# Two-layer products and seven-product groups in one stream on TensorE: the order of the units, a third waiting item and a fourth rotating bank

## The chip, the cores and the metric

The kernel runs on one core of a Trainium2 chip. The metric is the device time of one execution in microseconds (us). A core has TensorE (PE, matrix products; PEld is its weight load, which runs beside the products), VectorE (DVE), ScalarE (ACT), GpSimd (POOL) and SyncE (SP, which here issues most DMA transfers). Each engine works through its own instructions in the order in which they are written for it, and waits on semaphores for the others. Products are summed in PSUM, of which the kernel has eight banks of 128 x 512 fp32.

## The reference

```
X = fft(fft(x, axis=1), axis=2).real          # 8 batches of 3072 x 256
e = argmax(X @ w_gate)                        # one of 8 experts for each of 24576 tokens
y = scale * (relu(X @ w1[e]) @ w2[e])         # w1: 256 x 1024, w2: 1024 x 256
out = relu(y @ w_in) ** 2 @ w_out             # w_in: 256 x 2048, w_out: 2048 x 256
```

`scale` is the gate's probability times a sigmoid. All of it is fp32. The kernel splits every operand into a high and a low part (h and l) and forms each product as three: h by h, h by l, l by h.

## The kernel before

**Slots.** The Fourier transforms of the eight batches run first and scatter their tokens, sorted by expert, into a buffer `xs`. The rest works on slots of 256 tokens of one expert: 48 full ones (F) of the last window, 40 of earlier windows, and the tail slots (T), in which the experts' remainders lie. A unit is one slot's work in the first two layers; its output `y` is a tile of 128 x 512. The last window has 60 units, 48 F and 12 T, after batch eight.

**First two layers** (`items_a`, lines 634 to 668). Four items a unit. Each is `mm1` (12 products of 128x128 by 128x256 into a bank `ph`), `evac` (ACT relu into `hh`, DVE remainder `hl`) and `mm2` (12 products into `py`). After the fourth, ACT copies `py` to `ys`.

**The other two layers.** For the windows before the last: `items_c`, eight items a slot, relu and square (`squares`, lines 812 to 821), 12 products into `po`. In the last window two F slots make a pair, and `items_s` (line 753) computes the pair's third layer with seven products in place of eight (Strassen's way): eight steps, each `one` (12 products into two banks `px` and `pz2`, ACT copies `m`, DVE sums `u`, `z`, `x` on line 778), `two` (nine more products into the same banks, then `squares` on both) and two `last` (12 products each into `po`). That is 45 products a step, 360 a group. `inputs` (line 738) builds the group's operands `bh`, `bl` from two `ys`. The tail slots' outputs are summed up in DRAM (`yt`) and read back as four groups of two slots.

**Order.** The units of the last window are 24 F, then twelve times F, T, F. For each unit the loop in `run` first pushes the four items of the first two layers, then a share of the steps of the group whose slots came before. `push` lets `lag` = 2 items wait for their second half; `push_group` runs `one`, one waiting item, `two`, and leaves at most three waiting. A scheduler then moves single products among neighbours. After the last unit come `beyond` (line 940: a branch, not taken here, on the number of tail slots, PE's row L944), the last pair, and the four groups of tail slots with no first layers beside them.

**Weights.** An expert's `w1` and `w2` (1 MB each) land in single buffers `r1` and `r2`, issued by SP (lines 570 and 571) when the last split has read the buffer, and only when the expert changes (`chg`). `split_w(k)` (lines 582, 583) makes chunk k of four: ACT casts to `w1h` and `w2h`, POOL forms `w1l` and `w2l`. These too are single buffers, so that a cast for the next unit waits until PE has used the chunk. The load for the next unit stands in front of a unit's four items, the splits between the group steps behind them.

**Banks.** `ph`, `px` and every second `pz2` share three banks with the tag h; the other `pz2` have a bank of their own (tag fd). `py`, two `po` and one for transposes take the rest.

Of the kernel before, what the change touches and what calls it, by code (L numbers as in the profile page):

```python
# [10 lines left out]
F32 = mybir.dt.float32  # L11
# [3 lines left out]
U32 = mybir.dt.uint32  # L15
# [84 lines left out]
class Kern:  # L100
    def __init__(self, tc, a, B):
        self.tc, self.nc, self.a, self.B = tc, tc.nc, a, B
        self.L = B * S + SLOT
        self.sc_b, self.loads, self.outs = set(), False, False
        self.queue, self.lag, self.last_w = [], 2, None
        self.strassen = False
# [398 lines left out]
    def changes(self, *exs):  # L505
# [3 lines left out]
        if len(exs) == 1:  # L509
            m = exs[0]  # L510
        else:
            m = wp.tile([1, n], F32, name="exm", bufs=1)

            f, t = exs
            g = t.shape[1]
            h = f.shape[1] - 2 * g
            r = m[:, h:n].rearrange("p (g k) -> p g k", k=3)
            if h:
                v.tensor_copy(out=m[:, 0:h], in_=f[:, 0:h])
            v.tensor_copy(out=r[:, :, 0:3:2], in_=f[:, h:].rearrange("p (g k) -> p g k", k=2))  # L520
            v.tensor_copy(out=r[:, :, 1], in_=t)
# [86 lines left out]
    def ids(self, ids, scales):  # L608

        i = self.ap.tile([P, 2], U32, name="id", bufs=6)  # L610
        s = self.ap.tile([P, 2], F32, name="sc", bufs=6)
# [8 lines left out]

    def first(self, wh, wl, x, chunk):

        ph = self.ps.tile([P, 512], F32, name="ph", tag="h", bufs=3)
# [10 lines left out]
    def items_a(self, sl):  # L634
        st = {}
        for i in range(4):
# [10 lines left out]
            def mm2(i=i):  # L647
# [10 lines left out]
                if i == 3:  # L658
                    if self.strassen:
                        ys = self.yp.tile([P, 2, SLOT], F32, name="ys", tag="yl" if sl["tail"] else "yh", bufs=2)  # L660
# [92 lines left out]
    def items_s(self, b, ids):  # L753
# [10 lines left out]
        for g in range(8):  # L764
# [57 lines left out]

    def push_group(self, it):
        one, two, *last = it
        one()
        if self.queue:
            self.queue.pop(0)()
        two()
        self.queue += last
        while len(self.queue) > 3:  # L830
            self.queue.pop(0)()
# [18 lines left out]
    def run(self, units):  # L850
# [40 lines left out]
        groups = []  # L891
        for u in units[len(single):]:
            if not groups or (sum(not x["tail"] for x in groups[-1]) == 2 and not u["tail"]):
                groups.append([])
            groups[-1].append(u)
        self.strassen = True
        work = [(1, it) for it in self.items_c(pend)]
        first = True
        for group in groups:
            for k, u in enumerate(group):  # L900
                nxt = after.get(id(u))
                if nxt:
                    self.load(nxt) if "tab" in nxt else (nxt["open"](nxt), self.load(nxt))
                for it in self.items_a(u):
                    self.push(it)
                    yield
                n = -(-len(work) // (len(group) - k))
                part, work = work[:n], work[n:]
                todo = [lambda q=q: self.split_w(q) for q in range(4)] + [lambda: self.prep(nxt)] if nxt else []
                for q, (kind, it) in enumerate(part):  # L910
                    (self.push if kind == 1 else self.push_group)(it)
                    for _ in range(len(todo) if q == len(part) - 1 else kind if q else kind - 1):
                        if todo:
                            todo.pop(0)()
                    yield
                if first:
                    first = False
                    self.sums()
            pair = [u for u in group if not u["tail"]]
            while "y" not in pair[1]:  # L920
                self.queue.pop(0)()
            work = [(2, it) for it in self.items_s(self.inputs(pair[0]["y"], pair[1]["y"]), [u["id"] for u in pair])]
        self.flush()
        self.beyond(next(u["tab"] for u in units if u["tail"]))
        for kind, it in work:
            self.push_group(it)
        for m in range(self.n_tail // 2):
            y = [self.yp.tile([P, 2, SLOT], F32, name="ys", tag="yh", bufs=2) for _ in range(2)]
            ids = []
            for q in range(2):  # L930
                at = (2 * m + q) * SLOT
                self.nc.sync.dma_start(out=y[q], in_=self.yt[:, :, at:at + SLOT])
                raw = self.ap.tile([P, 2, 2], F32, name="rawid", bufs=2)
                self.nc.sync.dma_start(out=raw, in_=self.idt[at:at + SLOT, :].rearrange("(t p) o -> p t o", p=P))
                ids.append(self.ids(raw[:, :, 0], raw[:, :, 1]))
            for it in self.items_s(self.inputs(*y), ids):
                self.push_group(it)
        self.flush()
# [20 lines left out]
def build(ctx, tc, a, B, plan, pace=1.25):  # L959
# [54 lines left out]
    for w, (nb, n) in enumerate(plan):  # L1014
        kinds = [False] * n
        if w == len(plan) - 1:
            kinds = [False] * (n - 2 * KEEP) + [False, True, False] * KEEP
# [50 lines left out]
```

## Time and profile before

| what | value |
| --- | --- |
| median of three runs | 3784.23 us (3779.04 to 3785.14) |
| the profiled execution | 3785.43 us, its span 3783.8 us |
| PE, PEld | 3605.2 us (95%), 3528.7 us (93%) |
| ACT, DVE, POOL | 2412.7 us (64%), 2120.9 us (56%), 1585.8 us (42%) |
| DMA | 226.35 MB in packets, mean 60 GB/s |

PE's row in the page counts a matmul as busy until its modelled end, about 0.28 us after its start, while the next one starts about 0.12 us after it. Pauses shorter than that do not show as idle time. So this document measures PE by its count of matmuls: a stretch without any wait gives the time from one start to the next, and what a stretch takes beyond its count times that is pause. The last window's work on PE begins at about 1775 us. From there to about 2610 us the units are F alone, then F, T, F to about 3520 us, then the branch, the last pair and the four tail groups; the last store ends the span.

### The profile page before, as it was taken

Reading aid. Unit: us, or ns where it says so; the run is one execution under the profiler, and the core shown is the slowest. Engines: PE = TensorE matmul, PEld = TensorE weight load, DVE = VectorE, ACT = ScalarE, POOL = GpSimd, SP = SyncE. Lnnn points to the kernel's source line nnn. Section 1 sums busy time; section 2 is a strip of 40 time slices with the busy share of each in tenths; the row PEclk is TensorE's granted clock in tenths of the full one; section 3 lists DMA queues with packets and bytes.
Section 4 is the critical chain, followed back from the end, with each engine's and each line's share of the span. In section 5 each row is a group of like instructions: output and inputs, shape, how many; then the busy total and the mean of one; then the engine's idle time right before and its main releaser. Section 6 shows DMA issues by size and latency. Waiting matters only on the chain. (4 is left out here: it accounts for less than half of the span.)

```text
span 3783.8 us, 76706 instructions
## 1 busy us (share of the span) xinstructions
PE 3605.2 (95%) x29484; PEld 3528.7 (93%) x29484; DVE 2120.9 (56%) x4043; ACT 2412.7 (64%) x4793; POOL 1585.8 (42%) x1612
## 2 busy tenths in 40 slices
PE   4599999999999998999999999999999999999998
PEld 4588999999999998999999999999999999999888
DVE  8776666767676766333445545445444445444554
ACT  3455666665656565666667767767666677767565
POOL 4755455455444544333433433333544444444100
PEclk9799999999999999999999999999999999999999
DMA  5314222212121311011010101012221102100000
GB/s 188 131 50 135 65 95 83 93 65 90 60 96 38 109 47 63 16 66 37 22 34 15 40 15 39 20 57 65 79 99 64 45 29 81 64 21 18 24 24 12
DMA packets 157811, 226.35 MB, mean 60 GB/s; under 512 B 18560, under 2 KB 128384, under 8 KB 157440
## 3 DMA queue, kind: packets, MB, share of 16 engines
q1 hardware_dynamic: 137920, 166.46, 13.9%
q0 software_dynamic: 19520, 54.94, 4.0%
q8 instruction: 233, 3.82, 0.4%
q14 instruction: 138, 1.13, 0.1%
HBM read 288.79 MB, written 56.29 MB: 91 GB/s over the span
## 5 line engine op out<-in xcount | busy, mean ns | idle before, releaser
L618 PE MATMUL po<-woh,hl 128*128 128x256 f32 x3072 | 871.0, 285 | 28.1 <-DVE hl L820 28.1
L618 PE MATMUL po<-woh,hh 128*128 128x256 f32 x3072 | 864.1, 282 | 18.5 <-ACT hh L819 17.2
L618 PE MATMUL po<-wol,hh 128*128 128x256 f32 x3072 | 860.1, 281 | 4.2 <-POOL wol L411 4.2
L583 POOL TENSOR_TENSOR w1l<-r,w1h 128x512 fp32r<-128x512 f32 x400 | 523.7, 1313 | 727.9 <-ACT w1h L582 726.8
L583 POOL TENSOR_TENSOR w2l<-r,w2h 128x512 fp32r<-128x512 f32 x400 | 524.0, 1316 | 297.5 <-ACT w2h L582 284.6
L618 PEld LDWEIGHTS po<-woh,hl 128*128 128x128 f32 x3072 | 579.7, 189 | 48.3 <-DVE hl L820 48.0
L618 PEld LDWEIGHTS po<-woh,hh 128*128 128x128 f32 x3072 | 581.6, 189 | 20.9 <-ACT hh L819 19.3
L618 PEld LDWEIGHTS po<-wol,hh 128*128 128x128 f32 x3072 | 581.6, 189 | 5.0 <-POOL wol L411 4.9
L644 DVE SCALAR_TENSOR_TENSOR hl<-ph,hh 128x512 fp32r<-128x512 f32 x400 | 274.1, 688 | 439.6 <-ACT hh L643 438.8
L582 ACT CAST w1h<-r 128x512 fp32r<-128x512 f32 x400 | 246.7, 622 | 404.7 <-PE ph L618 382.7
L618 PE MATMUL py<-hl,w2h 128*128 128x256 f32 x1600 | 454.3, 284 | 16.0 <-DVE hl L644 15.8
L618 PE MATMUL ph<-xl,w1h 128*128 128x256 f32 x1600 | 456.1, 285 | 7.2 <-DVE xl L590 7.2
L618 PE MATMUL ph<-xh,w1h 128*128 128x256 f32 x1600 | 455.4, 285 | 1.2 <-ACT w1h L582 1.2
L618 PE MATMUL ph<-xh,w1l 128*128 128x256 f32 x1600 | 452.8, 283 | 1.4 <-POOL w1l L583 1.4
L618 PE MATMUL py<-hh,w2l 128*128 128x256 f32 x1600 | 451.4, 282 | 0.4 <-POOL w2l L583 0.4
L618 PE MATMUL py<-hh,w2h 128*128 128x256 f32 x1600 | 449.6, 281 | 0.0
L820 DVE TENSOR_TENSOR hl<-ph,hh 128x512 fp32r<-128x512 f32 x320 | 220.1, 688 | 375.9 <-ACT hh L819 375.7
L820 DVE TENSOR_TENSOR hl<-px,hh 128x512 fp32r<-128x512 f32 x224 | 155.0, 692 | 463.5 <-ACT hh L819 428.2
L618 PE MATMUL ph<-yh,wih 128*128 128x256 f32 x1280 | 369.5, 289 | 0.0
L618 PE MATMUL ph<-yl,wih 128*128 128x256 f32 x1280 | 360.7, 282 | 0.0
L618 PE MATMUL ph<-yh,wil 128*128 128x256 f32 x1280 | 360.7, 282 | 0.0
L815 ACT ACTIVATE rl<-ph 128x512 f32<-128x512 f32 x320 | 191.8, 600 | 256.4 <-PE ph L618 249.8
(279 smaller groups left out, 9822.3 us busy)
## 6 DMA issues: line engine op xcount, KB each, us to landing
r<-w SPq DMA_DIRECT2D x198, 1024.0 KB
xr<-xs SPq DMA_DIRECT2D x100, 260.0 KB
trig<-c_trig SPq DMA_DIRECT2D x104, 128.0 KB
X<-x SPq DMA_DIRECT2D x8, 1024.0 KB
X<-x SPq DMA_DIRECT2D x8, 768.0 KB
X<-x SPq DMA_DIRECT2D x8, 640.0 KB
conv<-w_in SPq DMA_DIRECT2D x16, 256.0 KB
conv<-w_out SPq DMA_DIRECT2D x16, 256.0 KB
```

The costliest lines, as they stand in the source:

```text
L582: nc.scalar.copy(out=h, in_=r)
L583: nc.gpsimd.tensor_tensor(out=l, in0=r, in1=h.bitcast(F32), op=ALU.subtract)
L618: self.nc.tensor.matmul(out=out, lhsT=l, rhs=r, start=first and i == 0, stop=last and i == len(pairs) - 1, skip_group_check=True)
L644: self.evac = self.nc.vector.scalar_tensor_tensor(out=l, in0=st[i], scalar=0.0, in1=h.bitcast(F32), op0=ALU.max, op1=ALU.subtract)
L815: self.nc.scalar.activation(out=r, in_=ps, func=AF.Relu)
L820: self.evac = self.nc.vector.tensor_tensor(out=l, in0=ps, in1=h.bitcast(F32), op=ALU.subtract)
```

## The change

1. `lag` is 3 instead of 2, for the whole kernel.
2. The units of the last window are twelve times F, T, F first, then 24 F.
3. Behind the first three units, pushes and `push_group` give way to `weave`: in each step of a group it writes `one`, the first waiting `last` of the step before, one `mm1`, `two`, the second `last` with any further `mm1`, and then the evacuation and `mm2` of the items taken. A plan says how many items a step takes. In the F, T, F part it is two ahead of the group and then 1, 2, 1, 1, 1, 2, 1, 1; in the F part two ahead and then 0, 1, 0, 1, 0, 1, 0, 1.
4. `stream` brings the weights: the load for the unit after the next one is written right behind a unit's fourth item, and each of the next unit's four splits behind an item's `mm2`.
5. `bank` gives `ph`, `px` and `pz2` four banks in rotation (three of tag h and fd).
6. `beyond` stands in the middle, between the F, T, F part and the F part. Before it the items in flight are finished; behind it the first unit's weights are loaded without a condition and split anew. The four tail groups stand between the pairs of the F part; the last pair alone has no first layers beside it.
7. `id` and `sc` get 10 buffers instead of 6, `ys` of odd slots a second tag, the tail groups' inputs the buffers of `ot`; the table of expert changes follows the new order.

The products are the same in number. The core of the diff (the bookkeeping in `changes` and `kinds`, and the code that goes out of `run`, left out):

```
-        self.queue, self.lag, self.last_w = [], 2, None
+        self.queue, self.lag, self.last_w = [], 3, None
...
+    def bank(self, name):
+        self.turn = (self.turn + 1) % 4 if self.woven else 0
+        tag, bufs = ("fd", 1) if self.turn == 3 else ("h", 3)
+        return self.ps.tile([P, 512], F32, name=name, tag=tag, bufs=bufs)
...
-                x = self.ps.tile([P, 512], F32, name="px", tag="h", bufs=3)
-                z = self.ps.tile([P, 512], F32, name="pz2", tag="fd" if g % 2 else "h", bufs=1 if g % 2 else 3)
+                x, z = self.bank("px"), self.bank("pz2")
...
+        for q in range(KEEP - 1):
+            self.weave(groups(q), a, [2] + [1, 2, 1, 1, 1, 2, 1, 1])
...
         self.beyond(next(u["tab"] for u in units if u["tail"]))
+        self.last_w = None
+        rest = late[3 * KEEP:]
+        a = self.stream(rest, True)
...
+            if m < self.n_tail // 2 and (need > done or q == len(rest) // 2 + KEEP - 1):
+                g, m = self.tails(m), m + 1
+            else:
+                done += sum(self.ahead(a, need - done))
+                g, q = groups(q), q + 1
+                plan = [0] + [0] * 4 + [1] * 4 if not done else [2] + [0, 1, 0, 1, 0, 1, 0, 1]
...
+    def stream(self, us, fresh=False):
+        def bring(u):
+            if u:
+                u["open"](u)
+                if u is us[0]:
+                    del u["chg"]
+                self.load(u)
+        if fresh:
+            bring(us[0])
+            for k in range(4):
+                self.split_w(k)
+            self.prep(us[0])
+        bring(us[1])
+        for u, nxt, far in zip(us, us[1:] + [None], us[2:] + [None, None]):
+            for i, (mm1, evac, mm2) in enumerate(self.items_a(u)):
+                def one(mm1=mm1, evac=evac, i=i, nxt=nxt):
+                    mm1()
+                    evac()
+                    if i == 3 and nxt:
+                        self.prep(nxt)
+                def two(mm2=mm2, i=i, nxt=nxt, far=far):
+                    mm2()
+                    if nxt:
+                        self.split_w(i)
+                    if i == 3:
+                        bring(far)
+                yield one, two
+    def weave(self, groups, a, plan):
...
+        for k in plan[1:]:
+            first, second, *last = it
+            first()
+            for f in self.pend[:1]:
+                f()
+            x = some(min(k, 1))
+            for i in x:
+                i[0]()
+            second()
+            for f in self.pend[1:]:
+                f()
+            y = some(k - 1)
+            for i in y:
+                i[0]()
+            for i in x + y:
+                i[1]()
+            self.pend = last
+            it = next(todo, None)
```

KEEP is 12 and n_tail 8. With these the groups are: 11 of the F, T, F part with 12 items each; the twelfth pair's group, beside which the fresh stream starts; then the tail groups and pairs 12 to 22 of the F part, the twelfth of them with the last items; and pair 23 alone.

Two places show what now stands in a row. The first is PE, in the F, T, F part, ahead of a step's second half (`px<-bh,wih` with the wait for DVE and ACT opens `two`; `po` are products of a waiting `last`, `ph` those of a first-layer item). Before:

```order
18222 L618 MATMUL po_32897<-woh_130,hh_32822 128x256
18223 L618 MATMUL po_32897<-wol_131,hh_32822 128x256
18224 L618 MATMUL po_32897<-woh_130,hl_32823 128x256
18225 L618 MATMUL px_32918<-bh_32582,wih_128 128x256 [waits PE_49]
18226 L618 MATMUL px_32918<-bl_32583,wih_128 128x256
18227 L618 MATMUL px_32918<-bh_32582,wil_129 128x256
18228 L618 MATMUL px_32918<-bh_32582,sh_23746 128x256
18229 L618 MATMUL px_32918<-bl_32583,sh_23746 128x256
18230 L618 MATMUL px_32918<-bh_32582,sl_23747 128x256
18231 L618 MATMUL pz2_32919<-bh_32582,sh_23746 128x256 [waits DVE_49,PE_49]
18232 L618 MATMUL px_32837<-bh_32582,wih_128 128x256 [waits DVE_49,Activation_49]
```

The same place after:

```order
14612 L617 MATMUL ph_26800<-xh_26469,w1l_135 128x256
14613 L617 MATMUL ph_26800<-xh_26469,w1h_134 128x256
14614 L617 MATMUL ph_26800<-xl_26470,w1h_134 128x256
14615 L617 MATMUL ph_26800<-xh_26469,w1l_135 128x256
14616 L597 MATMUL pt_26817<-ident_87,xr_26530 128x128 [waits DMAHW2_49]
14617 L597 MATMUL pt_26817<-ident_87,xr_26530 128x128 x3
14618 L617 MATMUL px_26764<-bh_26561,wih_128 128x256 [waits DVE_49,Activation_49]
14619 L617 MATMUL px_26764<-bl_26562,wih_128 128x256
14620 L617 MATMUL px_26764<-bh_26561,wil_129 128x256
14621 L617 MATMUL pz2_26765<-bh_26561,wih_128 128x256 [waits Activation_49]
14622 L617 MATMUL pz2_26765<-bl_26562,wih_128 128x256
```

Before, one waiting item of 12 products stood between the halves of a step, and what the scheduler could fetch from the next step. Now the 12 products of a `last` and the 12 of a `ph` stand there, and the next step's first half stays behind.

The second place is ACT around the first cast from a newly loaded `r2` (the wait on a DMAHW semaphore is the one for the load; line 582 is 581 after, 643 is 648, 815 is 819). Before:

```order
4338 L582 CAST w1h_134<-r1_132 128x2x256 [waits PE_49,Pool_49]
4339 L643 ACTIVATE hh_47074<-ph_47061 128x512 [waits PE_49]
4340 L582 CAST w2h_136<-r2_133 128x512 [waits DMAHW4_49,PE_49,Pool_49]
4341 L582 CAST w1h_134<-r1_132 128x2x256 [waits PE_49,Pool_49]
4342 L643 ACTIVATE hh_47104<-ph_47091 128x512 [waits DVE_49,PE_49]
4343 L582 CAST w2h_136<-r2_133 128x512 [waits PE_49,Pool_49]
4344 L779 COPY m_47134<-px_47120 128x256 [waits PE_49]
```

In the woven F, T, F part after:

```order
2333 L581 CAST w2h_136<-r2_133 128x512 [waits PE_49,Pool_49]
2334 L666 COPY ys_26900<-py_26611 128x512 [waits PE_49]
2335 L581 CAST w1h_134<-r1_132 128x2x256 [waits DMAHW7_49,Pool_49]
2336 L783 COPY m_26968<-px_26954 128x256 [waits PE_49]
2337 L786 COPY m_26972<-pz2_26955 128x256 [waits PE_49]
2338 L581 CAST w1h_134<-r1_132 128x2x256 [waits PE_49,Pool_49]
2339 L581 CAST w2h_136<-r2_133 128x512 [waits DMAHW0_49,Pool_49]
2340 L648 ACTIVATE hh_27001<-ph_26988 128x512 [waits DVE_49,PE_49]
2341 L819 ACTIVATE rl_27014<-px_26954 128x512 [waits DVE_49,PE_49]
```

The cast that frees `r2` (2333, the old expert's last chunk) and the one that needs its new content (2339) now stand six rows apart in the same queue, and the relu of the next `ph` and the step's squares stand behind the second one.

## Rows read from the trace of the kernel before

**Rows 1.** The page, busy time of each engine: us, share of the span, instructions.
```profile
PE 3605.2 (95%) x29484; PEld 3528.7 (93%) x29484; DVE 2120.9 (56%) x4043; ACT 2412.7 (64%) x4793; POOL 1585.8 (42%) x1612
```

**Rows 2.** Windows: from:to in us, length, then each engine's busy time.
```profile
core 0: us, PE busy (x) PEld busy (x) DVE busy (x) ACT busy (x) POOL busy (x), PEclk, DMA share, GB/s
...
400.00:1500.00 1100.00, 1059.07 (x8850) 1049.80 (x8850) 740.16 (x1448) 666.96 (x1320) 530.14 (x587) 0.98 0.24 77
1540.00:1760.00 220.00, 220.00 (x1872) 220.00 (x1871) 66.48 (x103) 141.49 (x243) 76.35 (x76) 1.00 0.14 47
1850.00:2630.00 780.00, 777.05 (x6353) 757.35 (x6352) 391.51 (x698) 543.95 (x1086) 285.94 (x271) 1.00 0.11 33
2630.00:3523.00 893.00, 891.01 (x7341) 874.33 (x7341) 425.38 (x746) 619.16 (x1216) 384.54 (x346) 1.00 0.17 56
3523.00:3572.00 49.00, 42.87 (x326) 40.58 (x325) 25.71 (x48) 29.55 (x63) 5.07 (x12) 0.97 0.09 23
3572.00:3776.00 204.00, 191.04 (x1513) 182.15 (x1511) 116.08 (x218) 134.72 (x284) 17.19 (x25) 1.00 0.06 19
3776.00:3784.00 8.00, 0.00 (x0) 0.00 (x0) 0.41 (x1) 0.00 (x0) 3.72 (x4) 0.69 0.18 66
```

**Rows 3.** PEld's waits, 1850 to 3523 us: us in total, times, longest.
```profile
PEld px L618 <- issue: 25.7, 123, 0.3
PEld po L618 <- DVE hl L820: 11.9, 66, 0.2
```

**Rows 4.** Timeline of PE at one such wait: start, us, line, operation.
```profile
2317.90 0.28 PE L618 MATMUL ph<-xh,w1l 128*128 128x256 f32 x1
2318.24 0.36 PE L618 MATMUL px<-bh,wih 128*128 128x256 f32 x1
2318.43 0.28 PE L618 MATMUL px<-bl,wih 128*128 128x256 f32 x1
```

**Rows 5.** Timeline of DVE just before it.
```profile
2317.66 0.43 DVE L778 TENSOR_TENSOR px<-pz,m 128x256 f32<-128x256 f32 x1
```

**Rows 6.** PE's waits, 3523 to 3784 us.
```profile
PE px L618 <- PEq L944: 3.8, 1, 3.8
```

**Rows 7.** Windows around the branch.
```profile
3531.00:3533.00 2.00, 0.00 (x0) 0.00 (x0) 0.75 (x2) 0.00 (x0) 1.63 (x2) 1.00 0.53 158
3533.00:3537.00 4.00, 3.82 (x19) 3.85 (x20) 0.99 (x2) 0.75 (x2) 2.49 (x6) 0.57 0.31 103
```

**Rows 8.** Windows: a tail group's middle, then the passage to the next group.
```profile
3634.00:3669.00 35.00, 33.97 (x272) 32.74 (x273) 18.69 (x35) 23.77 (x51) 4.61 (x8) 1.00 0.05 16
3669.00:3682.00 13.00, 11.46 (x90) 10.64 (x89) 8.84 (x18) 8.21 (x19) 0.00 (x0) 1.00 0.15 42
```

**Rows 9.** Timeline of SP, the issue of a load of r2.
```profile
2720.37 0.37 SPq L571 DMA_DIRECT2D r<-w  x1
```

**Rows 10.** Windows over that load.
```profile
2720.00:2726.50 6.50, 6.50 (x57) 6.50 (x56) 5.46 (x12) 6.25 (x13) 0.34 (x1) 1.00 0.64 206
```

**Rows 11.** Waits of ACT over the whole run, the row for a load.
```profile
ACT w1h L582 <- DMA r<-w: 6.6, 2, 3.4
```

**Rows 12.** Lines by form, 1800 to 3400 us: busy us, mean ns of one.
```profile
L583 POOL TENSOR_TENSOR w2l<-r,w2h 128x512 fp32r<-128x512 f32 x213 | 274.5, 1293 | 208.0 <-ACT w2h L582 200.7
...
L582 ACT CAST w2h<-r 128x512 fp32r<-128x512 f32 x212 | 134.4, 634 | 82.5 <-PE py L618 67.6 <-issue 14.6 <-POOL w1l L583 0.3
...
L643 ACT ACTIVATE hh<-ph 128x512 fp32r<-128x512 f32 x214 | 128.7, 601 | 0.0
...
L820 DVE TENSOR_TENSOR hl<-px,hh 128x512 fp32r<-128x512 f32 x171 | 118.3, 692 | 359.9 <-ACT hh L819 328.3 <-PE ph L618 29.3
```

**Rows 13.** PE's waits, 150 to 1800 us.
```profile
PE po L618 <- DVE hl L820: 27.9, 15, 5.4
...
PE po L618 <- ACT hh L819: 10.3, 3, 8.3
PE py L618 <- DVE hl L644: 9.4, 7, 4.8
```

More of the change, by code (lines that the diff above doesn't have):

```diff
@@ L104, in __init__ @@
         self.sc_b, self.loads, self.outs = set(), False, False
-        self.queue, self.lag, self.last_w = [], 2, None
-        self.strassen = False
+        self.queue, self.lag, self.last_w = [], 3, None
+        self.strassen = self.woven = self.both = False
+        self.turn = 0
     def setup(self, cp, fp, st, ps, dp):
@@ L659, in mm2 @@
                     if self.strassen:
-                        ys = self.yp.tile([P, 2, SLOT], F32, name="ys", tag="yl" if sl["tail"] else "yh", bufs=2)
+                        ys = self.yp.tile([P, 2, SLOT], F32, name="ys", tag="yl" if sl["tail"] or self.both and sl["i"] % 2 else "yh", bufs=2)
                         self.nc.scalar.copy(out=ys, in_=st["y"].rearrange("p (c t) -> p c t", c=2))
@@ L821, in squares @@
         return h, l
[L823 to L831, printed above, removed]
     def push(self, it):
@@ L890, in run @@
                 yield
[L891 to L895, printed above, removed]
-        self.strassen = True
[L897 to L922, printed above, removed]
@@ L923, in run @@
-        self.flush()
-        self.beyond(next(u["tab"] for u in units if u["tail"]))
[L925 to L937, printed above, removed]
@@ L938, in run @@
-        self.flush()
+        late = units[len(single):]
+        self.strassen = True
+        group, rest = late[:3], late[3:3 * KEEP]
+        work = list(self.items_c(pend))
+        for k, u in enumerate(group):
+            nxt = after[id(u)]
+            self.load(nxt) if "tab" in nxt else (nxt["open"](nxt), self.load(nxt))
+            for it in self.items_a(u):
+                self.push(it)
+                yield
+            n = -(-len(work) // (len(group) - k))
+            part, work = work[:n], work[n:]
+            todo = [lambda q=q: self.split_w(q) for q in range(4)] + [lambda: self.prep(nxt)]
+            for q, it in enumerate(part):
+                self.push(it)
+                for _ in range(len(todo) if q == len(part) - 1 else 1 if q else 0):
+                    if todo:
+                        todo.pop(0)()
+                yield
+            if k == 0:
+                self.sums()
@@ new lines, in run @@
+        self.flush()
+        self.woven, self.turn, self.pend = True, -1, ()
+        pair = lambda q: [u for u in late if not u["tail"]][2 * q:2 * q + 2]
+        groups = lambda q: lambda: self.items_s(self.inputs(*(u["y"] for u in pair(q))), [u["id"] for u in pair(q)])
+        a = self.stream(rest)
+        for q in range(KEEP - 1):
+            self.weave(groups(q), a, [2] + [1, 2, 1, 1, 1, 2, 1, 1])
+            yield
+        assert next(a, None) is None
+        for last in self.pend:
+            last()
@@ new lines, in run @@
+        self.pend = ()
+        self.beyond(next(u["tab"] for u in units if u["tail"]))
+        self.last_w = None
+        rest = late[3 * KEEP:]
+        a = self.stream(rest, True)
+        self.both = True
+        q, m, done = KEEP - 1, 0, 0
+        for _ in range(len(rest) // 2 + self.n_tail // 2 + 1):
+            need = 8 * (q + 1 - KEEP)
+            if m < self.n_tail // 2 and (need > done or q == len(rest) // 2 + KEEP - 1):
[4 more added lines that the diff above has]
+                plan = [0] + [0] * 4 + [1] * 4 if not done else [2] + [0, 1, 0, 1, 0, 1, 0, 1]
+            if q == len(rest) // 2 + KEEP - 1 and m == self.n_tail // 2:
+                plan = [2] + [1] * 8
+            done += self.weave(g, a, plan)
+            yield
@@ new lines, in run @@
+        for last in self.pend:
+            last()
+    def stream(self, us, fresh=False):
[25 more added lines that the diff above has]
+                yield one, two
@@ new lines, in weave, with some @@
+    def weave(self, groups, a, plan):
+        n = 0
+        def some(k):
+            nonlocal n
+            got = [x for x in (next(a, None) for _ in range(k)) if x]
+            n += len(got)
+            return got
+        todo = iter(groups())
+        it = next(todo)
+        for x in self.ahead(a, plan[0]):
+            n += x
+        for k in plan[1:]:
[16 more added lines that the diff above has]
+            it = next(todo, None)
+        return n
@@ new lines, in ahead, with tails @@
+    def ahead(self, a, k):
+        held = []
+        for _ in range(k):
+            x = next(a, None)
+            if x:
+                x[0]()
+                held.append(x)
+                yield 1
+        for x in held:
+            x[1]()
+    def tails(self, m):
+        y = [self.yp.tile([P, 2, SLOT], F32, name="yb", tag="ot", bufs=2) for _ in range(2)]
+        ids = []
+        for q in range(2):
+            at = (2 * m + q) * SLOT
+            self.nc.sync.dma_start(out=y[q], in_=self.yt[:, :, at:at + SLOT])
+            raw = self.ap.tile([P, 2, 2], F32, name="rawid", bufs=2)
+            self.nc.sync.dma_start(out=raw, in_=self.idt[at:at + SLOT, :].rearrange("(t p) o -> p t o", p=P))
+            ids.append(self.ids(raw[:, :, 0], raw[:, :, 1]))
+        return lambda: self.items_s(self.inputs(*y), ids)
@@ L1016, in build @@
         if w == len(plan) - 1:
[L1017 removed]
+            kinds = [False, True, False] * KEEP + [False] * (n - 2 * KEEP)
         c = [0, 0]
```

14 lines of the change are left out of this document (6 added, 8 removed).

## The prediction

> **What bounds the kernel now.** I read the page's busy times first: PE is busy 95% of the span, ACT 64%, POOL 42% [rows 1]. So the time is PE's products plus PE's pauses, and since the products are the same in number after the change, only pauses can move. The second view is the windows [rows 2]: 1540 to 1760 us holds 1872 products in 220.00 us without a gap, which makes a ruler of 0.1175 us from start to start. Laid on the last window's stretches, it gives these pauses. 1850 to 2630 us (F units): 780 - 6353 x 0.1175 = 33.5 us. A group there has 360 products, two slots' 192 and 8 transposes, 560 in all, so that is 11.3 groups and 3.0 us of pause each. 2630 to 3523 us (F, T, F; 660 in a group): 893 - 7341 x 0.1175 = 30.4 us over 11.1 groups, 2.7 us each. 3523 to 3572 us (branch, last pair): 49 - 326 x 0.1175 = 10.7 us. The four tail groups alone: 204 - 1513 x 0.1175 = 26.2 us, 6.5 us each. With twelve groups of each of the first two kinds this makes 12 x 3.0 + 12 x 2.7 + 10.7 + 26.2 = 105 us that the weaving can work on. The final 8 us without PE [rows 2] stay: both kernels end with a group and its stores.
>
> The third view says what the small pauses are. PEld stands 123 times for 0.2 us at `px` and 66 times at `po` for `hl` [rows 3]. The first is put down to nothing visible; the timeline shows it: PE starts a product at 2317.90, should start the next 0.12 later and starts it at 2318.24 [rows 4]; DVE ended `px<-pz,m` at 2318.09 [rows 5]. So `two` comes up to PE before the chain ACT `m`, DVE `u`, `z`, `x` is through: each such miss costs some 0.2 us, and 0.08 more behind the first product (0.19 instead of 0.12 [rows 4]).
>
> **The order within a step.** Before, 12 products of a waiting item stood between `one` and `two`, 1.4 us; the chain needs about 1.7. After, a step with an item has 24 between them, 2.8 us, so this wait should go. The `po` products wait for `hl`: of the step before, 12 `last`, 12 `py` and 12 of `one` now cover 4.2 us, against relu, square, cast and subtraction, each 0.60 to 0.69 like the relu and the subtraction of [rows 12], on `px` and `pz2` in turn, some 3.4 us with the start. I charge steps with one item 0.1 us. A step without an item has 12 to 15 products there and is like the middles of the tail groups: 35 - 272 x 0.1175 = 3.0 us over six steps of 45 products, 0.5 each [rows 8]. Bounds 0 and 0.5; I take 0.3, nearer the row, since three products of `last` now slip in between.
>
> **The loads.** This is what the change adds. The load of `w2` can be issued once POOL has made the last `w2l` from the old content; now the first cast from the new content stands six rows behind in ACT's queue, ahead of the next relu. Worked out from the end of the fourth `py`: 0.3 us to start, cast 0.63, POOL 1.29 [rows 12], the transfer, cast 0.63, relu 0.60, DVE 0.69. The transfer: issued at 2720.37 [rows 9]; the window to 2726.5 moved 206 GB/s, 1.34 MB, which is the 1 MB and a slot's tokens of 0.26 MB [rows 10], so at most 6.1 us; I take 5.2. Sum 9.3 us. PE has 69 products until it needs that `hl`, 8.1 us. So PE is 1.2 us late where the expert changes (2.1 with 6.1 us, nothing where it does not). By the data 26 of the 33 units in this part change the expert, about nine at this one of a group's three boundaries: 1.1 us a group with what follows. At the other two boundaries the second cast comes a step later, and I charge nothing. The start of a group, where `inputs` puts casts and subtractions ahead of its first `one`, 0.8 us: the passage between tail groups costs 13 - 90 x 0.1175 = 2.4 us [rows 8] with nothing beside it, and now 24 products of two items taken ahead, 2.8 us, stand there, though part of the casts comes behind them. Bounds 0 and 2.4.
>
> So a group of the F, T, F part: 8 x 0.1 + 0.8 + 1.1 = 2.7, less 0.1 for the steps with two items: 2.6 us. Eleven of them: 28.6. A group of the F part: 4 x 0.3 + 4 x 0.1 + 0.8 = 2.4 us, thirteen of them with the tail groups that now have items beside them: 31.2.
>
> **The middle and the end.** `beyond` costs 3.8 us of PE standing still [rows 6] and then a stretch at the lower clock: 3533 to 3537 us holds 19 products at a granted clock of 0.57, so mostly at the lower of its two levels (1.2 of 2.4 GHz), 4.0 - 19 x 0.1175 = 1.8 us lost [rows 7]. These two stay, and move. Before the branch the items in flight are finished: 2 us. Behind it the fresh load runs without cover for ACT, whose queue holds the casts ahead of the squares: eight casts of 0.63 make 5 us, of which I count 3, and of the transfer 4.9: together 15.5 us, where the old place with the last pair had 10.7. The first tail group behind it has items only in its second half: 5.5. The pair with eight items and the last pair alone, which is like a tail group with its drain: 3.2 and 9.2. The entry into the weave: 2. After: 2 + 28.6 + 15.5 + 5.5 + 31.2 + 3.2 + 9.2 = 95 us against 105: 10 us gained. The new unit order by itself is free where the load is hidden; its price is in the 1.1 us. Buffers of `id`, `sc`, `ys` only take waits away, on engines that are not the bound: nothing.
>
> **The third waiting item.** Before 1510 us PE waits for `hl` and `hh` 25 times, 47.6 us [rows 13], in bursts in which ACT or DVE work for a transform. With one item more PE has 12 products, 1.4 us, of slack more in each, never more, since `ph` has three banks and the third next `mm1` waits for the same `hl`. Bounds 0 and 25 x 1.0 (many are shorter than 1.4); long waits (up to 8.3) only lose 1.4 once. I take half, 12 us. The price is one chunk of weights held 1.4 us longer, under POOL's and ACT's idle time.
>
> **Sum.** 10 + 12 = 22 us off the profiled execution, 3785.4 (span 3783.8): 3763.4. The median of the three runs is 1.2 us lower than that execution: 3762.
>
> **Rivals.**
> Loads take over (slower). The load now has to land within a step, and ACT's queue is in order: relu, `m` and squares of the running step stand behind a cast that waits. ACT has waited for a load before, twice, up to 3.4 us [rows 11]. If all 26 changes in the F, T, F part cost that much, 88 us in place of the 12 charged: 3838. It turns slower from about 0.85 us more for each change than I charge. Against it: the `w1` half is issued a block earlier. For it: all the slack of the old order, where the load stood in front of four items, is gone.
>
> Pauses nearly vanish. Loads hidden (1.1 x 11 = 12 us), starts of groups and steps without items at half (13 x 0.9 = 12), the branch 3 less, third item at 20: 3762 - 12 - 12 - 3 - 8 = 3727. For it: the small waits are all of one kind, and short.
>
> Pauses only move. The third item gives nothing, since bursts on ACT are longer than its slack, and steps without items cost the row's 0.5 (52 x 0.2 = 10 us): 3784, no change.
>
> The clock. The only fall of the granted clock in the last window comes behind the long pause at the branch [rows 7]; with three rotating banks and 0.2 us pauses it stays 1.00 [rows 2]. If each of the 28 woven or tail groups had one fall of 1.8 us, 50 us: 3812. The Trainium skill ("TensorE: Matmul & The Clock Gate", section "A second HAM failure mode: psum-queue depth-cycling") tells of a kernel whose cycling through PSUM banks let PE idle briefly and the clock move between its two levels; by that rule the fourth bank in rotation would be a price, while the trace disagrees so far for three banks at 1.00.
>
> That the change does not do what it says is ruled out: the order of the products is the one described.
>
> **How the numbers follow.** Forecast 3762 (3745 to 3776): 0.43. Pauses vanish: 0.16. Only move: 0.16. Loads take over: 0.21, half of it above 3805. Clock: 0.04. The range reaches down to 3722 and up to 3805, and leaves out some 0.06 below and 0.13 above. A measurement of this kernel tells 0.2%, 7.6 us, from no change: faster 0.43 + 0.16 = 0.59, within 0.16, slower 0.25.
>
> **What would show it.** In the changed trace the 0.2 us waits at `px` should be gone from steps with items; a window over the F, T, F part should show 2.6 us of pause a group by the ruler, and ACT rows waiting for a load of `r` should be near 1 us or absent. Rows of several us there mean the loads rival. Before 1510 us, waits for `hl` should be down by about a quarter. A granted clock under 1.00 outside the branch would mean the clock rival. The forecast fails most easily at the transfer's time and at the start behind the branch, which no row of before shows under these conditions.

## The result and the profile after

The changed kernel takes 3738.69 us (median of four runs, 3735.01 to 3744.75) against 3784.57 us of the kernel before in the same comparison: a ratio of 0.9884, 95% interval 0.9866 to 0.9901. That is 46 us less. The forecast was 3762, 22 us less, with a range of 3722 to 3805. So the sign and the range held, and the forecast size was half of what came.

The page after, busy times (compare [rows 1]): the products are the same in number, and PE is busy for 96%.

```profile
PE 3579.7 (96%) x29484; PEld 3515.6 (94%) x29484; DVE 2128.3 (57%) x4043; ACT 2368.8 (63%) x4793; POOL 1605.8 (43%) x1612
```

Where the time went shows at one landmark that both kernels have, ACT's first copy of `py` to `ys` in the last window. Timeline of ACT, before and then after:

```profile
1774.80 0.59 ACT L661 COPY ys<-py 128x512 f32<-128x512 f32 x1
```

```profile
1723.07 0.59 ACT L666 COPY ys<-py 128x512 f32<-128x512 f32 x1
```

The profiled execution after took 3744.75 us (span 3743.1), the one before 3785.43 (3783.8). Up to the landmark the changed kernel gains 51.7 us. From there to the end it takes 2020.0 us instead of 2009.0: the woven part loses 11. (The profiled execution after is 6 us above its median, so the loss in a middling run may be smaller; where those 6 us lie is not known.)

Windows after, by the prediction's ruler of 0.1175 us a product: nine woven F, T, F groups, the group at the branch, eleven groups of the F part with the tail groups among them. The columns are those of [rows 2].

```profile
1845.30:2581.20 735.90, 723.30 (x5942) 709.25 (x5941) 351.50 (x604) 487.13 (x991) 326.25 (x289) 1.00 0.25 81
2661.60:2729.80 68.20, 61.83 (x473) 60.22 (x472) 33.05 (x62) 43.93 (x91) 25.26 (x30) 0.92 0.19 60
2852.20:3542.90 690.70, 682.60 (x5617) 669.25 (x5616) 373.06 (x654) 472.77 (x981) 222.95 (x217) 1.00 0.09 26
```

F, T, F: 735.9 - 5942 x 0.1175 = 37.7 us over nine, 4.2 a group (forecast 2.6, before 2.7). The branch's group: 68.2 - 473 x 0.1175 = 12.6 (forecast 15.5). F part: 690.7 - 5617 x 0.1175 = 30.7 over eleven, 2.8 a group (forecast 2.4). Summed from each group's first `bh` to the next, the last window has 117 us of pause, where the forecast had 95 and the kernel before 104.

And the early part, to about 1500 us. PE's waits from 150 to 1800 us after (compare [rows 13]), the three that answer to the old ones; and, from the same view of before, the one for the gate's product `pp`:

```profile
PE ph L617 <- DVE hl L824: 25.3, 10, 7.1
...
PE ph L617 <- DVE hl L649: 2.6, 1, 2.6
PE pp L308 <- DVE oh L302: 1.7, 4, 0.6
```

```profile
PE pp L307 <- DVE oh L301: 11.0, 5, 4.4
```

The wait for `hl` has moved from `po` and `py` to `ph`, as the prediction said for three banks; 47.6 us in 25 waits have become some 28 in 11, and the wait of `pp`, 11.0 us before, is 1.7. One wait grew: `pz` for POOL's `X`, 1.5 us before, takes 6.6.

### The profile page after: what moved, and what is told of

It is laid out like the page before. It is cut to its first block, busy times and chain, and to the rows that moved or that the text cites. A ratio compares the mean times of both kernels' runs of the same rounds, so it can differ in the third digit from the quotient of the medians.

```text
span 3743.1 us, 76757 instructions
## 1 busy us (share of the span) xinstructions
PE 3579.7 (96%) x29484; PEld 3515.6 (94%) x29484; DVE 2128.3 (57%) x4043; ACT 2368.8 (63%) x4793; POOL 1605.8 (43%) x1612
## 5 line engine op out<-in xcount | busy, mean ns | idle before, releaser
L582 POOL TENSOR_TENSOR w1l<-r,w1h 128x512 fp32r<-128x512 f32 x400 | 545.4, 1368 | 864.2 <-ACT w1h L581 861.0
```

The source lines that it names most:

```text
L582: nc.gpsimd.tensor_tensor(out=l, in0=r, in1=h.bitcast(F32), op=ALU.subtract)
```

## The experiments

All are compared with runs of the kernel before on the same chip. "First ys" is the landmark above.

**1. The third waiting item alone**, in the kernel before:

```
-        self.queue, self.lag, self.last_w = [], 2, None
+        self.queue, self.lag, self.last_w = [], 3, None
```

> The kernel before with three waiting items instead of two and nothing else. In the trace of the changed kernel the first ys of the last window is copied at 1723.1 us, in that of before at 1774.8: 51.7 us earlier, while the rest of the run takes 2020.0 us against 2009.0. Theory: the third item alone gives the 52 us, and the weaving costs 11: this kernel is near 3733, faster than both. Rival: the early gain comes from the ten buffers of id and sc or from the other order of the code, and the weaving pays: then this kernel is near 3770 to 3784.

Measured: 3736.78 us, ratio 0.9869 (0.9853 to 0.9886). The landmark:

```profile
1724.00 0.59 ACT L661 COPY ys<-py 128x512 f32<-128x512 f32 x1
```

One number gives 48 us, all that the whole change gave. In the last window of the old order the third item helps the F groups and costs the others. Windows over eight F groups (546.6 - 4482 x 0.1175 = 20.0, 2.5 each against 3.0) and nine F, T, F groups (731.5 - 5942 x 0.1175 = 33.3, 3.7 each against 2.7):

```profile
1890.10:2436.70 546.60, 544.66 (x4482) 533.94 (x4482) 278.13 (x497) 378.82 (x770) 201.00 (x192) 1.00 0.08 24
2666.50:3398.00 731.50, 727.95 (x5942) 710.36 (x5941) 346.47 (x604) 503.24 (x992) 320.75 (x288) 1.00 0.18 56
```

**2. The weaving with two waiting items**, in the changed kernel:

```
-        self.queue, self.lag, self.last_w = [], 3, None
+        self.queue, self.lag, self.last_w = [], 2, None
```

> The changed kernel with two waiting items as before. Theory: it is the weaving alone, about 11 us slower than before: 3795, with the first ys of the last window back near 1775 us. Rival (weaving or buffers bring the gain): 3738 to 3760.

Measured: 3798.36 us, ratio 1.0034 (1.0023 to 1.0046). The landmark:

```profile
1774.19 0.59 ACT L666 COPY ys<-py 128x512 f32<-128x512 f32 x1
```

The weaving alone is 14 us slower than the kernel before. Beside the third item it costs 2 us by the medians (3738.69 against 3736.78, in different comparisons), which can't be told from nothing.

**3. No expert loads in the woven part**: the condition of the load is never true, and ACT casts what lies there.

```
-    ... cond=q.value_load(u["chg"], min_val=0, max_val=1) > 0)
+    ... cond=q.value_load(u["chg"], min_val=0, max_val=1) > (1 if self.woven else 0))
```

> The changed kernel with the condition of the expert loads in the woven part never true: those transfers are left out, the casts work on old content, the result is wrong. The groups of the F, T, F part have 4.2 us of pause now by the ruler of 0.1175 us, 2.75 before. Theory: the loads make some 2 us of it: a group falls to about 2.2, the whole by 11 x 2.0 = 22 us and a little in the F part, to about 3715. Rival: the loads are hidden and the pause is the start of a group and ACT's order: less than 5 us, 3734 to 3738.

Measured: 3723.28 us, ratio 0.9829 (0.9812 to 0.9845): 15 us under the changed kernel, between the two that were expected. Nine F, T, F groups:

```profile
1845.30:2566.20 720.90, 714.81 (x5942) 707.12 (x5941) 352.36 (x604) 486.73 (x990) 327.39 (x288) 1.00 0.07 21
```

720.9 - 5942 x 0.1175 = 22.7, 2.5 a group instead of 4.2: the loads cost 1.7 us a group, and what is left is the start of a group and the steps. How it comes about can be read in the changed kernel at a boundary of two units. SP's issue of `w2`, POOL's last remainder ahead of it, ACT's casts and relu, and PE's products:

```profile
2116.43 0.37 SPq L570 DMA_DIRECT2D r<-w  x1
```

```profile
2115.11 1.29 POOL L582 TENSOR_TENSOR w2l<-r,w2h 128x512 fp32r<-128x512 f32 x1 [4.48 <-ACT w2h L581]
```

```profile
2114.41 0.62 ACT L581 CAST w2h<-r 128x512 fp32r<-128x512 f32 x1 [0.70 <-PE py L617]
...
2121.80 0.62 ACT L581 CAST w2h<-r 128x512 fp32r<-128x512 f32 x1 [0.86 <-DMA r<-w]
2122.32 0.59 ACT L648 ACTIVATE hh<-ph 128x512 fp32r<-128x512 f32 x1
```

```profile
2122.55 0.28 PE L617 MATMUL po<-woh,hl 128*128 128x256 f32 x1
2122.97 0.38 PE L617 MATMUL py<-hh,w2h 128*128 128x256 f32 x1
2123.70 0.39 PE L617 MATMUL py<-hl,w2h 128*128 128x256 f32 x1 [0.34 <-DVE hl L649]
```

The load is issued when POOL is through, the cast starts 5.4 us later, the relu behind it. PE stands for `hh` at 2122.97 and once more for `hl` at 2123.70. Beyond the ruler these two starts are 0.3 and 0.6 us late, 0.9 together: the prediction's chain, step by step. In the whole last window ACT waited 25 times for a load, 29.6 us in all:

```profile
ACT w2h L581 <- DMA r<-w: 25.8, 19, 2.7
ACT w1h L581 <- DMA r<-w: 3.8, 6, 1.7
```

**4. Later splits**, so that a load has an item more before its first cast:

```
-                    if nxt:
-                        self.split_w(i)
+                    for k in ((), (0,), (1, 2), (3,))[i] if nxt else ():
+                        self.split_w(k)
```

> The changed kernel with the splits of the next unit's weights behind the items 1 (chunk 0), 2 (chunks 1 and 2) and 3 (chunk 3) instead of one behind each: a new load has one item more, 6 to 8 us, before ACT's first cast from it. If the loads are what makes the F, T, F groups long, their pause falls from 4.2 to about 2.5 and the run to about 3720. If the price is in the number of casts ahead of the relu, two chunks together make it worse: 3738 to 3750.

Measured: 3733.45 us, ratio 0.9863 (0.9846 to 0.9879). This misses the 3720 expected. The F, T, F groups do fall to 2.7 us; in the F part half of the groups rise from 2.9 to 4.1, where every second step has no item and two chunks are now cast at once; why that costs more there was not tried. The next experiment keeps the later splits where they helped.

**5. Later splits in the F, T, F part alone**:

```
-                    if nxt:
-                        self.split_w(i)
+                    for k in (((i,) if fresh else ((), (0,), (1, 2), (3,))[i]) if nxt else ()):
+                        self.split_w(k)
```

> The changed kernel with the later splits in the F, T, F part alone; the F part keeps one split behind each item. In the run with later splits everywhere the F, T, F groups fell from 4.2 to 2.7 us of pause, and half the later groups rose from 2.9 to 4.1. So 15 us off the changed kernel: near 3724, 12 us under the kernel with the third item alone. If what the F, T, F part gains is given back behind the branch: 3733.

Measured: 3720.04 us, ratio 0.9838 (0.9822 to 0.9855): the fastest version that leaves nothing out, 64 us under the kernel before and, by the ratios, 17 under the changed one and 12 under the third item alone. So with the loads covered the weaving does gain, if little: behind the first ys this run takes 2002.7 us and experiment 1 takes 2011.4, and the intervals of the two ratios just touch. Its nine F, T, F groups hold 723.4 - 5942 x 0.1175 = 25.2 us, 2.8 each, and ACT's longest sum of waits for loads is halved. (The profiled executions differ by 24.9 us; 7.6 of them lie ahead of the first ys, where the code is the same, so what the later splits give is better read from the groups.) The nine groups, and ACT's wait:

```profile
1835.90:2559.30 723.40, 716.95 (x5942) 708.10 (x5941) 351.49 (x603) 486.06 (x991) 327.48 (x289) 1.00 0.25 82
```

```profile
ACT w2h L581 <- DMA r<-w: 12.6, 7, 2.2
```

**6. No middle**: one stream through all groups, no draining, no branch, no fresh load.

```
-        group, rest = late[:3], late[3:3 * KEEP]
+        group, rest = late[:3], late[3:]
...
-        for last in self.pend:
-            last()
-        self.pend = ()
-        self.beyond(next(u["tab"] for u in units if u["tail"]))
-        self.last_w = None
...
-        a = self.stream(rest, True)
```

> The changed kernel without the branch, the draining ahead of it, the fresh load and the eight splits behind it: one stream of items runs through all groups (the branch is not taken on these inputs, so the output stays). By the ruler the group in the middle holds 13.0 us of pause and the next one 4.4, against 2.3 to 3.5 for the groups after. If the middle costs what the forecast said, some 10 to 12 us go, and some 4 more that the first tail group loses: 3725 to 3728. If the pauses only move (the loads in the middle then wait as in the F, T, F part), 3734 to 3739.

Measured: 3734.89 us, ratio 0.9878 (0.9862 to 0.9895). The medians differ by 4 us and the intervals overlap, so the time alone does not show a gain. The middle group, from its first `bh` to the next group's, in the changed kernel and here:

```profile
2660.00:2729.30 69.30, 62.93 (x482) 61.32 (x482) 33.89 (x64) 45.00 (x95) 24.99 (x29) 0.93 0.19 59
```

```profile
2658.30:2717.90 59.60, 57.01 (x466) 55.41 (x465) 33.10 (x61) 39.89 (x84) 14.34 (x14) 1.00 0.08 23
```

Its pause falls from 12.7 to 4.8 us by the ruler, but the next group's stays at 4.5. So the middle is worth up to 8 us, less than the 10 to 14 expected.

**7. Three banks in rotation**:

```
-        self.turn = (self.turn + 1) % 4 if self.woven else 0
+        self.turn = (self.turn + 1) % 3 if self.woven else 0
```

> The changed kernel with three banks in rotation instead of four for ph, px and pz2. A step takes three banks with one item and four with two. If the fourth bank matters, each step waits for the remainder hl of the step before ahead of its own one: 1 us or more in each of 28 x 8 steps, 3850 or above. If the weave has slack enough without it, 3739 to 3760. The clock rival of the forecast would show here as a granted clock under 1.00 in the woven part, at either number.

Measured: 3786.07 us, ratio 1.0014 (1.0004 to 1.0023), between the two ranges expected. The fourth bank is worth 47 us in this order. The first window is the F, T, F part, where nothing changes (37.8 us in nine groups); the second is the F part, 690.7 - 5423 x 0.1175 = 53.5 us of pause where there were 30.7 with 194 products more:

```profile
1845.30:2581.20 735.90, 725.13 (x5941) 710.21 (x5941) 351.28 (x603) 488.36 (x990) 327.31 (x288) 1.00 0.25 81
2852.20:3542.90 690.70, 674.88 (x5423) 651.20 (x5422) 366.98 (x636) 460.27 (x947) 218.47 (x213) 1.00 0.08 26
```

The granted clock is 1.00, the higher of its two levels, with three banks and with four.

**8. The splits of the earlier windows spread out**, in the kernel before:

```
-                if 1 <= k <= 3:
-                    self.split_w(k - 1)
-                    if k == 3:
-                        self.split_w(3)
+                if k % 2:
+                    self.split_w(k // 2)
```

> The kernel before, two waiting items, with the four splits of the earlier windows behind the second, fourth, sixth and eighth step instead of behind the second, third and (two) fourth. In the trace of before a DVE addition of two SBUF tiles takes 8.19 us at 981.12, as long as seven splits of POOL stand without a pause, and the next hl comes behind it. Theory: what the third item covers is these stretched additions; with splits in twos they are at most some 3 us long, and the first ys comes 20 to 50 us earlier than 1774.8 without a third item: 3735 to 3765. Rival: the waits come from the transform's own chain on DVE and ACT: 3780 to 3785.

Measured: 3782.13 us, ratio 0.9996 (0.9987 to 1.0006). Nothing, but it did not try the theory: POOL's row at the same place, behind the scatter of `out`, was as long as before (six remainders, not the seven of the expectation), and the DVE addition took 8.18 us again.

**9 and 10. POOL's work cut**, with two waiting items and with three: in the windows before the last, POOL forms each remainder over 32 of 256 columns (the rest is left out; `first` is true the first time that a chunk is split).

```
+            if not (first or self.strassen):
+                r, h, l = r[:, :, 0:32], h[:, :, 0:32], l[:, :, 0:32]
             nc.gpsimd.tensor_tensor(out=l, in0=r, in1=h.bitcast(F32), op=ALU.subtract)
```

> The kernel before (two waiting items) with POOL's remainder of each weight chunk formed over an eighth of its columns in the windows before the last; seven eighths of that work are left out and the result is wrong. Spreading the splits left the long rows of POOL as they were (they queue behind the scatter of out), so the theory of the stretched additions was not tried by it. Theory: without long rows on POOL the DVE additions stay near 0.7 us, PE's waits for hl go, and the first ys of the last window comes at 1725 to 1750 instead of 1774.8: 3735 to 3760. Rival, the waits come from the number of transform operations ahead of the hl on DVE and ACT: 3780 to 3785.

> The same with three waiting items. If the third item covers the stretched additions and little else, this kernel is where the one with short POOL operations and two items is, and no more than 10 us under the kernel with the third item alone (3736.8). If the two are separate, both gains add: 3705 to 3720.

Measured: 3699.13 us (ratio 0.9775, 0.9759 to 0.9792) with two, 3699.59 (0.9777, 0.9761 to 0.9794) with three. First ys, two and then three:

```profile
1691.84 0.60 ACT L666 COPY ys<-py 128x512 f32<-128x512 f32 x1
```

```profile
1686.59 0.59 ACT L666 COPY ys<-py 128x512 f32<-128x512 f32 x1
```

With POOL out of the way the early part is 83 us shorter, and the third item gives nothing more to the run: 5 us ahead of the landmark, lost again behind it. What it covers, then, is what POOL's long operations do to the early part. Both expectations had a smaller gain, though: the run is 37 us faster than with the third item alone, so the third item covers only part of it. What POOL's operations do can be seen at a transform's addition on DVE in the kernel before, then POOL and PE beside it:

```profile
980.41 0.68 DVE L160 TENSOR_TENSOR X<-X 128x512 f32<-128x512 f32 x1
981.12 8.19 DVE L157 SCALAR_TENSOR_TENSOR X<-X 128x512 f32<-128x512 f32 x1
989.23 0.68 DVE L820 TENSOR_TENSOR hl<-ph,hh 128x512 fp32r<-128x512 f32 x1
```

```profile
981.27 1.31 POOL L583 TENSOR_TENSOR w1l<-r,w1h 128x512 fp32r<-128x512 f32 x1
982.52 1.32 POOL L583 TENSOR_TENSOR w2l<-r,w2h 128x512 fp32r<-128x512 f32 x1
983.77 1.31 POOL L583 TENSOR_TENSOR w1l<-r,w1h 128x512 fp32r<-128x512 f32 x1
985.02 3.73 POOL L583 TENSOR_TENSOR w2l<-r,w2h 128x512 fp32r<-128x512 f32 x3
```

```profile
986.27 0.28 PE L618 MATMUL po<-wol,hh 128*128 128x256 f32 x1
989.97 0.39 PE L618 MATMUL po<-woh,hl 128*128 128x256 f32 x1 [3.42 <-DVE hl L820]
```

An addition of this shape that takes 0.68 us takes 8.19 while POOL works through six remainders in a row; the `hl` that PE waits for comes behind it, and PE's next product starts 3.70 us after the last. Between 200 and 1520 us the kernel before has 34 DVE operations over 2 us, 148 us in all; with POOL's work cut there is none. Of the 87 us that PE pauses in this stretch, 41 lie within a DVE operation of over 1.3 us or in the 1 us behind it; with the change it is 13 of 36 (to 1469 us, the same product). Over 400 to 1400 us the group of the transform's additions of this shape, before and in experiment 9:

```profile
L157 DVE SCALAR_TENSOR_TENSOR X<-X 128x512 f32<-128x512 f32 x75 | 78.4, 1052 | 1.2
```

```profile
L158 DVE SCALAR_TENSOR_TENSOR X<-X 128x512 f32<-128x512 f32 x65 | 45.0, 698 | 1.1
```

The cut also lets `r1` and `r2` come free sooner and shortens POOL's own queue, and those shares were not measured apart. So the stretched operations account for some 41 us directly, and the 83 are an upper bound.

**11. Three items ahead of a group** instead of two, on top of experiment 5:

```
-            self.weave(groups(q), a, [2] + [1, 2, 1, 1, 1, 2, 1, 1])
+            self.weave(groups(q), a, [3] + [1, 1, 1, 2, 1, 1, 1, 1])
...
-                plan = ... [2] + [0, 1, 0, 1, 0, 1, 0, 1]
+                plan = ... [3] + [0, 1, 0, 1, 0, 1, 0, 0]
...
-                plan = [2] + [1] * 8
+                plan = [3] + [1] * 8
...
+            if n == 2 and self.pend:
+                self.pend[0]()
+                self.pend = self.pend[1:]
```

> The kernel with later splits in the F, T, F part, and three items instead of two ahead of each group's first half, the first last of the step before between the second and the third. At the start of a group PE stands 1.2 to 1.4 us for bl. If that is for want of products, 12 more (1.4 us) take most of it: some 1 us in each of 27 groups, 3692 to 3705. If the chain of inputs is only pushed back by the third item's relu and remainder, nothing: 3718 to 3724; and fewer items in the steps cost something.

Measured: 3730.77 us, ratio 0.9857 (0.9841 to 0.9874), 10 us slower than without, which neither expectation had. In the trace the F part's groups fall from 2.9 to 2.7 us, not by 1; one F, T, F group has 8.8 us, where a relu stands behind a late load; and the first ys comes at 1725.7, 10 us later than in experiment 5, although that part of the program is the same. The first ys of kernels with the same early code lies between 1715.5 and 1725.7, so this run can't price the third item ahead closely. The gain of 27 us is ruled out.

**12. The remainders on DVE** in the windows before the last, on top of experiment 5; nothing left out:

```
-            nc.gpsimd.tensor_tensor(out=l, in0=r, in1=h.bitcast(F32), op=ALU.subtract)
+            (nc.gpsimd if self.strassen else nc.vector).tensor_tensor(out=l, ...)
```

> The kernel with later splits in the F, T, F part, and in the windows before the last the remainders of the weights formed by DVE instead of POOL: nothing is left out. With POOL's rows gone the DVE additions stay short; against that DVE gets eight operations of 0.7 us more for each slot of some 34 us. If the stretched additions are what is left of the early waits, the first ys comes at 1690 to 1700 instead of 1715.5: 3695 to 3705. If a DVE operation that waits for ACT's cast, which waits for PE, stands ahead of hl in the queue, PE waits more than before: 3725 or above.

Measured: 3748.64 us on a chip where the kernel before takes 3806.47, ratio 0.9859 (0.9839 to 0.9878), no better than experiment 5's 0.9838 (the expected times were for the other chips). No DVE operation is above 1.3 us, but the queue has a new stop: remainders that wait for ACT's cast, and PE waits for the transform instead. DVE's wait, then PE's, 200 to 1469 us:

```profile
DVE w1l L582 <- ACT w1h L581: 43.6, 45, 5.2
```

```profile
PE pd L281 <- ACT zh L273: 11.9, 5, 4.6
```

So taking the conflict away is worth at most the 83 us of experiment 9, and this is not the way to take them.

## Why the prediction was right in sign and half in size

Two terms were wrong, in opposite directions: the third item was sized at 12 us and gives 48 (experiment 1); the weaving was to gain 10 and loses 2 to 14 (experiments 1 and 2). The errors partly cancel, so that the measured time lies within the range is in part luck.

*The third waiting item.* The step that failed is the sizing by "0 and 25 x 1.0", of which half was taken. The listed waits for `hl` and `hh` fell by 20 us, within that bound; but the bound was taken for the whole gain, and most of the gain lies elsewhere. Measured over the early part, before and after to the same product:

```profile
200.00:1520.00 1320.00, 1262.42 (x10494) 1246.57 (x10495) 891.67 (x1782) 792.98 (x1576) 642.16 (x707) 0.98 0.24 78
```

```profile
200.00:1469.00 1269.00, 1241.60 (x10495) 1229.46 (x10495) 867.58 (x1780) 786.64 (x1575) 646.45 (x706) 0.99 0.25 81
```

1320 - 10494 x 0.1175 = 87 us of pause before, 36 after. Of the 51, starts that lie more than 0.26 us behind the last give 34. Starts 0.20 to 0.26 us behind it, 403 before and 252 after, give 15; some 200 of them in either run fall where the clock is granted in full, and the 187 before and 53 after that fall at the lower of its two levels make 13 of the 15. This share was not in the sum: [rows 7] shows that the clock falls behind a pause, and [rows 2] had a mean of 0.98 in most of this stretch, but the fall was charged only to the branch. And the gate's `pp`, which waits for the same DVE queue, gave 9 more. The mechanism itself (12 products of slack, the wait then moving to `ph`) was as described, but the cause of the waits was not asked for. Had the DVE rows beside a wait been read, the 8.19 us addition would have shown that such a burst is one long hold.

*The chain within a step.* Right: in woven steps the 0.2 us waits at `px` are mostly gone (in the F, T, F part PE's waits there list 0.5 us for `px` on DVE's sums), and what is left is at the boundaries. In the F part, where every second step has no item, PEld still stands 39 times for 0.2 us at `px` between 2852 and 3543 us, as the 0.3 us charged for such steps allows.

*The loads.* Right in mechanism, short in size: 1.7 us a group for 1.1. The forecast charged one boundary of three; there the starts of `py` are 0.8 to 1.3 us late, at the others up to 0.4 us. As a rival ("Loads take over") it was too big: 25 waits of 1.2 us in the mean, not 3.4.

*The start of a group.* 0.8 us forecast; without loads a whole group is 2.5 us, of which the start takes some 1.3. PE waits for the last `bl`, nine times in the F, T, F part:

```profile
PE px L617 <- DVE bl L748: 5.5, 9, 0.6
```

The two items ahead don't cover the chain of `inputs`, which the old order covered with four.

*Middle and end.* 12.6 us for 15.5 in the branch's group, and 4.4 for 5.5 behind it: sizes held roughly. The F part's 2.8 for 2.4 is the start of a group again.

*The other rivals.* "Pauses nearly vanish" did not happen in the last window; the time came near it for another reason. "Pauses only move" is what the weaving did by itself. The clock rival fell: the granted clock is 1.00 in the windows of both woven parts, and 0.92 only in the branch's group. The Trainium skill's rule on cycling through PSUM banks ("TensorE: Matmul & The Clock Gate", section "A second HAM failure mode: psum-queue depth-cycling") shows in no row here, and the fourth bank is worth 47 us instead of costing.

## What to carry to other kernels

When a change to a waiting depth touches the whole kernel, size it from the pauses of the whole stretch (span less count times pace), not from the listed waits, and add the slower clock behind each pause. Ask of a long wait what held the engine in front of it: the operation before it in the same queue, and what ran beside that. In a woven order look for the boundary whose chain has too few products to cover it: here a load that is issued and needed within one step cost more (1.7 us a group) than the small waits that the weaving removed, and with the casts an item later the weaving gained some 9 us (experiment 5 against 1).

## What the runs showed of the hardware

A DVE addition with two inputs in SBUF stood still for as long as POOL worked through a row of operations, 8.19 us beside six remainders of 1.3 us; fifteen DVE operations of the early part took 4 to 9 us, eleven of them the transform's additions. The Trainium skill says ("SBUF — State Buffer", sections "Who interferes with whom" and "Summary: rules for kernel authors") that a DVE instruction with two SBUF inputs contends with a GpSimd instruction that reads SBUF, and that the second one to issue blocks until the first is through. The trace agrees as to these operations: the transform's additions read SBUF twice and stretch, while `hl`, which reads PSUM and SBUF, never takes over 0.69 us, not in the 103 cases that overlap a remainder on POOL either. As to the order the trace differs: by the records the addition began at 981.12, 0.15 us ahead of the first remainder, and yet it waited for the whole row. It is not always so. At 340 us the two engines take turns, and there it is POOL's remainders that are stretched, from 1.3 to 2.3 us:

```profile
339.80 2.27 POOL L583 TENSOR_TENSOR w1l<-r,w1h 128x512 fp32r<-128x512 f32 x1
342.03 2.25 POOL L583 TENSOR_TENSOR w2l<-r,w2h 128x512 fp32r<-128x512 f32 x1
```

What decides between the two is not shown. What the conflict costs this kernel is at most the 83 us of experiment 9, more than any version tried here gains.
